# A retention and channel-mix kernel on one core: its steps in a new order, the last columns halved, the first load in one transfer, ten zero products for twelve

## The chip, the cores and the metric

One core of a Trainium2 chip runs the whole kernel in one launch. The metric is the device time of one execution in microseconds. TensorE is PE below, VectorE DVE, ScalarE ACT, GpSimd POOL and SyncE SP; a weight load that belongs to a product is PEld.

## The reference, cut to what matters

Retention over 4 batches, 8 heads, 768 tokens and 64 columns a head, in blocks of 64 tokens, then a channel mix over the 512 columns of all heads:

```python
for b in range(12):                                    # blocks of 64 tokens
    intra = (qb @ kb.T * Dmask) @ vb                   # Dmask[i, j] = lam**(i - j) for i >= j
    out[block b] = intra + (qb * lam_pow) @ kv_state
    kv_state = lam**64 * kv_state + (kb * rev_pow).T @ vb
x_prev = x shifted by one token
xk = mu_k * x + (1 - mu_k) * x_prev                    # 512 columns
xr = mu_r * x + (1 - mu_r) * x_prev
k = relu(xk @ w_k)                                     # 1024 columns
r = sigmoid(xr @ w_r)
result = r * ((k * k) @ w_v)                           # 512 columns
```

The three weights arrive in float64, all else in float32.

## The kernel before, in words

**Tiling.** Two blocks make a stage of 128 tokens, so there are six stages n = 0 to 5. Heads are taken in pairs hp = 0 to 3, and all four batches go together. Attention gives x with its columns on partitions, one tile [128 columns, 4 x 128 tokens] a head pair. Weights, x and the squares of k are split into two parts, a high and a low one, and each product of the channel mix runs three times (`product`, `PASSES`): high by high, high by low, low by high.

**Attention** of a stage and head pair (short products of 64 x 64, 16 of a kind): `scores` (tile sc), `decay` (times the table Dt, DVE), `decay_queries`, `decay_keys` (ACT, in place in tile in or kin), `sums` (tile u), `even_state` and `odd_state` (the running state), `values` (tile xp). Then `mix_prev` and `mix` make xk and xr, and `split_x` the two parts (xh, xl). A stay in attention below is a run of such short products in PE's list, between long runs of the others: from stage 1 on mostly the values of two head pairs and the scores and sums of two others.

**Channel mix** of a stage: 48 products for r (`r_part`, tile rp, 6 by 4 rows of the order) and the sigmoid `r_out`; 96 for k (`k_part`, tile kp, eight tiles of 128 columns) with `k_square` and `k_split` (tile k); 96 for v (`v_part`, tile vp), whose result DVE multiplies by r (tile rt) and ACT's queue stores (`v_cols`). In stage 0 k is made head pair by head pair (`k_product`), as x comes. The last block of all (stage 5, batch 3) is computed and stored in two pieces of its columns (lines 462 and 463).

**Weights** come as float64 through SP's queue (`stage_part`, tile raw) and are turned into the two float32 parts on the chip, during stage 0: `conv_top` (ACT, tile top), `conv_bits` (DVE), `conv_split` (ACT writes wk, wr or wv, DVE the low part).

**Start.** The inputs of stage 0 come in pieces of a tile of 2048 columns for each head pair (keys twice, queries, values), cut at the columns of `CUTS` (line 503), issued by SP in the steps L, N and M (`load_first`). Small constants (smalls, eye) come first; from them DVE, POOL, ACT and PE make the table Dt and the tile LP (`powers`, steps T0 and T2). PE begins with products of zeros that nobody reads (`keep_busy`, step Z). Line 173 runs a Sigmoid on one column, with nothing behind it that reads the result.

**Order.** The string `ORDER` (from line 505) is the whole program: each word is a step, a letter (the table `steps`, lines 483 to 490), a stage, a tile or a weight, and a head pair or a part. Each step issues its instructions on their engines, and every operation goes through `InOrder` (line 25), which keeps each engine, and each queue, in the order of the program. So the order of this string is the order of each engine's list, and all instructions carry line 33. Loads are issued by SP (steps L, N, M, S), stores by ACT.

Of the kernel before, what the change touches and what calls it, by code (L numbers as in the profile page):

```python
# [7 lines left out]
F32 = mybir.dt.float32  # L8
F32R = mybir.dt.float32r
I32 = mybir.dt.int32  # L10
U32 = mybir.dt.uint32
# [3 lines left out]
AF = mybir.ActivationFunctionType  # L15
# [6 lines left out]
NF = DFF // 128  # L22
# [14 lines left out]
def tile_retention_moe(  # L37
# [25 lines left out]
    tensor, vector, scalar, gpsimd, sync = (  # L63
        InOrder(tc, e) for e in (tc.nc.tensor, tc.nc.vector, tc.nc.scalar, tc.nc.gpsimd, tc.nc.sync))
# [37 lines left out]
    def load_first(hp, part):  # L102
        cuts = CUTS[hp]
        part = min(part, len(cuts) - 2)
        if hp not in first:
            t = big.tile([128, 2048], F32, tag=f"big{hp}", name="in")
            first[hp] = t
            views((0, hp), [None] + [t[:, c * 512:c * 512 + 512] for c in (0, 2, 1, 3)])
        sync.dma_start(first[hp][:, cuts[part]:cuts[part + 1]], qvk0[hp, :, cuts[part]:cuts[part + 1]])
# [33 lines left out]
    one = tiny.tile([128, 1], F32, name="one")  # L143
# [10 lines left out]
    gpsimd.tensor_tensor(pows[:, 3:6], lam1.broadcast_to([128, 3]), ecol, op=ALU.pow)  # L154
    gpsimd.tensor_tensor(PW, lrow, prow.broadcast_to([128, H]), op=ALU.pow)
    gpsimd.tensor_tensor(KD, lrow, erow.broadcast_to([128, H]), op=ALU.pow)

    last, now, then = lam1, impulse, steps8
    for i in range(3):
# [10 lines left out]
    vector.tensor_tensor(rows.rearrange("p (c a) -> p c a", a=8), now[:, 8:25].rearrange("p (c o) -> p c o", o=1).broadcast_to([128, 17, 8]),  # L170
                         lows.rearrange("p (o a) -> p o a", o=1).broadcast_to([128, 17, 8]), op=ALU.mult)
    vector.tensor_scalar(omu, mus, -1.0, 1.0, op0=ALU.mult, op1=ALU.add)
    scalar.activation(one, one, AF.Sigmoid)
    gpsimd.memset(lastw, 0.0)
    gpsimd.tensor_copy(lone[:, 512:640].rearrange("p (a x) -> p a x", a=2),
                       parity.rearrange("p (a o) -> p a o", o=1).broadcast_to([128, 2, 64]))
# [231 lines left out]
    def product(p, stationary, moving, first, last):  # L408
        for i, (s, m) in enumerate(PASSES):
            tensor.matmul(p, stationary[s], moving[m], start=first and i == 0, stop=last and i == len(PASSES) - 1)  # L410

    def w_of(kind, i, c, cols):
        return [W[f"{kind}{i}"][:, c, s, cols] for s in (1, 0)]
# [43 lines left out]
    def v_part(n, i):  # L457
        b, half = divmod(i, 2)
        last = (n, b) == (NT - 1, B - 1)


        fs, cols = (range(half * 4, half * 4 + 4), slice(0, 512)) if not last else (
            range(NF), slice(half * 384, 384 + half * 128))
        if half == 0 or last:
            vps[n, b] = ps_m.tile([128, 512], F32, tag="m", name="vp")
        p = vps[n, b]
        for f in fs:
            x = k2[f // 2][:, f % 2, :, b * 128:b * 128 + 128]
            product(p[:, cols], [x[:, 0], x[:, 1]], w_of("v", f // 2, f % 2, cols),
                    f == 0, f == NF - 1)  # L470
        if last:
            v_cols(n, b, cols)

    def v_cols(n, b, cols):
        o = rt[b][:, cols]
        vector.tensor_tensor(o, vps[n, b][:, cols], o, op=ALU.mult)
        scalar.dma_start(out[b, n * 128:n * 128 + 128, cols], o)

    def v_out(n, b):
# [7 lines left out]
        y=lambda n, hp: split_x(n, 0, hp), x=lambda n, hp: split_x(n, 1, hp),  # L487
        M=lambda n, hp: load_first(hp, 2), b=keep_raw, G=lambda f, hp: k_product(0, f, hp),
        R=lambda n, hp: r_part(n, hp, 0), Q=lambda n, hp: r_part(n, hp, 1), s=r_out, K=k_part, h=k_square, p=k_split, V=v_part, o=v_out,
        S=stage_part, c=conv_top, C=conv_bits, D=conv_split)  # L490
    for step in ORDER.split():
# [8 lines left out]

CUTS = ((0, 1024, 1536, 2048), (0, 1536, 2048), (0, 1536, 2048), (0, 1536, 2048))

ORDER = """
L00 N00 M00 Z12 M02 T0 A00 a00 k00 B00 L02 Sk5 k02 Sk4 A02 b00 e00 E00 T2 a02 B02 F00 ck5 f00 L01 ck4 A01 Ck4 L03 x00 y00 e02
b02 Ck5 a01 Sk6 U00 Dk4 A03 M03 E02 a03 Dk5 Sk7 B01 u00 ck6 k03 G00 G20 e01 b01 Sk2 f02 Sk3 f01 ck7 E01 Ck7 G30 Ck6 B03 y01 y02
U02 Dk6 ck2 G10 G01 F01 G21 e03 b03 M01 Sr0 Sr1 f03 G31 Sr2 G11 ck3 k01 Ck2 G02 G22 G32 Ck3 Dk7 y03 Dk2 U01 u01 x01 G12 N11 G13
G03 Dk3 U03 cr0 Cr0 G23 h00 K07 Sr3 h01 F02 cr1 G33 E03 F03 Cr1 p00 h02 Dr0 cr2 h07 cr3 Cr2 Dr2 N10 Sv0 K05 x03 Sv3 Dr1 Cr3 h03
K06 K04 h06 x02 Sv1 p01 Dr3 q11 cv0 Q00 cv3 Cv0 h05 Cv3 h04 Dv0 L11 u03 cv1 Q01 u02 L10 Q02 Cv1 Dv3 Q03 k11 q10 R00 R01 Sv2 R02  # L510
R03 A10 s02 A11 k10 U11 Dv1 cv2 Cv2 U10 s00 p02 Dv2 V04 L12 p03 V02 s03 u11 a10 u10 k12 V05 N12 s01 a11 V03 L13 B11 B10 E11 w10
w11 N13 k13 A12 A13 e10 N21 N20 o02 o01 U13 U12 L21 E10 q12 L20 F11 u12 a13 V06 u13 q13 a12 V07 w13 k20 o03 V00 e11 f10 F10 w12
B13 x10 B12 A20 f11 k21 E13 x11 U21 A21 y10 U20 y11 L23 e12 e13 f12 F13 L22 V01 f13 y12 N22 y13 K13 N23 u21 q20 K15 E12 o00 k23
x13 h13 F12 w21 u20 q21 h15 K11 a21 K12 K14 a20 K10 k22 h14 p12 B20 x12 w20 h12 e20 f20 B21 A22 U22 q22 e21 U23 L30 h11 E20 A23
h10 F20 E21 Q10 Q11 Q12 Q13 u22 q23 w22 s12 f21 K17 F21 a23 p10 h17 u23 K16 R10 L31 s13 a22 R11 w23 y20 R12 R13 h16 x21 s10 k30
k31 B23 B22 N30 N31 p11 q31 A30 U30 A31 U31 y21 e23 E23 s11 F23 p13 L32 u30 e22 u31 N33 V10 f22 k32 V11 V14 a30 V15 f23 V12 x20
o10 L33 y22 V13 q30 y23 o12 K22 a31 x23 K25 E22 o11 K23 w31 h22 F22 K24 w30 N32 k33 V16 h23 V17 B30 h24 B31 U32 A32 h25 A33 q32
o13 U33 K27 x22 e30 e31 K26 f30 p22 N41 L40 E30 F30 K21 L41 h27 u32 u33 E31 K20 w32 f31 F31 h26 Q20 p21 Q21 h21 h20 k41 k40 Q22
Q23 q33 R20 R21 p20 a32 s22 V22 N40 w33 R22 a33 R23 y30 A40 p23 U40 U41 A41 s21 B32 y31 s20 q41 B33 s23 e33 f33 V23 V26 V27 x30
L43 o21 e32 a40 f32 y33 N43 E32 x31 V20 q40 u40 o23 y32 E33 V21 o20 F32 F33 K35 L42 h35 k42 Q30 N42 w40 Q31 K31 a41 h31 x33 V24  # L520
K34 u41 V25 x32 h34 p32 Q32 o22 K37 K30 w41 Q33 h37 h30 k43 B41 p30 e41 E41 B40 s32 E40 A43 f41 s33 U43 F40 A42 U42 u43 L51 K36
a42 N50 e40 f40 K33 q42 h36 R30 a43 h33 K32 u42 R31 q43 L50 N51 F41 k50 R32 R33 k51 B43 h32 p33 y40 p31 y41 s31 B42 s30 x40 E43
U50 e43 F43 U51 e42 x43 f42 y42 A51 f43 u51 A50 V32 L52 V33 y43 V36 o31 K44 V34 x41 N52 E42 F42 V37 q50 x42 K40 a51 h44 h40 o33
V30 V35 K41 u50 N53 V31 K45 h41 q51 h45 a50 p42 L53 w42 K47 o30 K46 p40 h47 K42 h46 Q40 h42 k52 o32 w43 K43 p43 B51 k53 h43 B50
e50 E51 f50 e51 A53 U53 f51 U52 E50 A52 Q41 y51 u52 Q42 F50 Q43 F51 R40 q53 R41 s43 p41 s42 R42 a52 x50 R43 s40 q52 V42 y50 s41
u53 V43 B52 a53 B53 e52 x51 f52 V46 E52 o41 F52 V47 e53 E53 y52 f53 V40 V44 V41 o40 y53 o43 V45 F53 K52 h52 R50 o42 K51 h51 K50
K53 x53 x52 R51 h53 h50 p51 R52 K54 K55 R53 h55 s50 s51 p50 h54 Q50 K57 p52 Q51 h57 V54 Q52 K56 h56 Q53 V50 p53 s52 V52 V53 V51
V55 s53 o51 o50 o52 V56 V57
"""


# [58 lines left out]
```

## Time and profile before

| | before |
|---|---|
| time, median of 3 runs | 403.63 us (403.32 to 403.79) |
| profiled execution | 403.18 us, its span 401.4 us |
| busy share of the span | PE 98%, PEld 81%, DVE 61%, ACT 51%, POOL 7% |
| chain that ended last | PE 86%, ACT 8%, DMA 4%, issue 1% |
| loaded and stored | 35.74 MB read, 6.29 MB written |
| granted TensorE clock, mean | 1.000 |

The span runs from the first to the last instruction, so the execution's own time is 1.8 us longer. Times in the rows are microseconds from the start of the span. The chain follows the work that ended last back to the start, from each piece to what released it. "issue" is time in which an engine waited for nothing that the profile shows. "SPq" and "ACTq" are an engine's DMA queue, L33 is line 33. A group of rows gives, for instructions of one kind, output <- inputs, count, busy time and mean duration, and the idle time before them with what ended it.

### The profile page before, as it was taken

How to read it: one execution, taken by the hardware profiler on the slowest of the kernel's cores; microseconds unless marked ns; L12 is line 12 of the kernel's file. 1: busy time of each engine (PE TensorE's matmuls, PEld its weight loads, DVE VectorE, ACT ScalarE, POOL GpSimd, SP SyncE). 2: the span in 40 equal slices, each digit the busy share in tenths (PEclk: the TensorE clock that was granted, in tenths of full speed). 3: DMA queues.
4: the chain of work that ended last, by engine and by line, in shares of the span. 5: the costliest groups of instructions: out<-in, count | busy, mean ns of one | idle time of the engine just before them, and what ended most of it. 6: DMA issues, size and time to landing. Idle time of an engine off the chain costs nothing.

```text
span 401.4 us, 8419 instructions
## 1 busy us (share of the span) xinstructions
PE 392.3 (98%) x3534; PEld 323.7 (81%) x3534; DVE 244.7 (61%) x392; ACT 206.0 (51%) x372; POOL 28.8 (7%) x100
## 2 busy tenths in 40 slices
PE   7899999899999999999999999999999999999997
PEld 3677877788888788888888888888888888888886
DVE  5897699887895783359575448755366941434111
ACT  5899998665657731186342445941237540224200
POOL 5221000010010100010100000000000000000000
PEclk9999999999999999999999999999999999999999
DMA  7999256927070710160261008080000000200011
GB/s 263 418 371 301 124 212 181 284 77 198 2 206 9 208 55 28 40 198 0 73 165 54 2 28 209 4 235 1 26 28 28 2 26 2 79 0 2 0 52 54
DMA packets 13318, 42.58 MB, mean 106 GB/s; under 512 B 1888, under 2 KB 2272, under 8 KB 13280
## 3 DMA queue, kind: packets, MB, share of 16 engines
q1 hardware_dynamic: 9536, 35.68, 28.5%
q10 hardware_dynamic: 3744, 6.36, 4.3%
q8 instruction: 28, 0.46, 0.5%
q14 instruction: 10, 0.08, 0.1%
HBM read 35.74 MB, written 6.29 MB: 105 GB/s over the span
## 4 chain that ended last, share of the span: by engine, by line
PE 86%; ACT 8%; DMA 4%; issue 1%; SPq 0%; DVE 0%; POOL 0%; ACTq 0%; POOLq 0%
PE vp L33 33%; PE kp L33 27%; PE rp L33 15%; PE xp L33 5%; DMA in<-qvk 4%; PE sc L33 3%; PE u L33 2%; ACT kf L33 2%; ACT top L33 2%; ACT xh L33 1%; ACT wk L33 1%; ACT ts L33 1%; ACT wr L33 0%; ACT in L33 0%; SPq L33 0%
## 5 line engine op out<-in xcount | busy, mean ns | idle before, releaser
L33 PE MATMUL vp<-wv,k 128*128 128x512 f32 (+2 forms) x600 | 136.0, 384 | 1.1 <-issue 1.1
L33 PEld LDWEIGHTS vp<-wv,k 128*128 128x128 f32 x600 | 110.0, 188 | 23.1 <-issue 1.4
L33 PE MATMUL kp<-xh,wk 128*128 128x512 f32 x384 | 123.0, 391 | 0.0
L33 PEld LDWEIGHTS kp<-xh,wk 128*128 128x128 f32 x384 | 72.1, 188 | 15.4 <-issue 0.2
L33 PE MATMUL kp<-xl,wk 128*128 128x512 f32 x192 | 74.9, 390 | 0.1
L33 ACT ACTIVATE kf<-kp 128x512 f32<-128x512 f32 x48 | 28.1, 594 | 75.9 <-PE kp L33 70.0
L33 PE MATMUL rp<-wr,xh 128*128 128x512 f32 x192 | 59.7, 392 | 0.2 <-ACT kf L33 0.2
L33 DVE TENSOR_TENSOR kf<-kf 128x512 f32<-128x512 f32 x40 | 27.1, 690 | 53.0 <-ACT kf L33 52.7
L33 DVE TENSOR_TENSOR xl<-ts,xh 128x512 fp32r<-128x512 f32 x48 | 32.6, 688 | 24.7 <-ACT xh L33 24.3
L33 ACT CAST xh<-ts 128x512 fp32r<-128x512 f32 x48 | 29.0, 617 | 30.4 <-DVE rt L33 26.2
L33 ACT COPY qv<-st 64x256 f32<-64x256 f32 x80 | 32.4, 405 | 20.6 <-DVE st L33 17.8
L33 PEld LDWEIGHTS rp<-wr,xh 128*128 128x128 f32 x192 | 35.6, 188 | 8.5 <-ACT kf L33 1.2
L33 PEld LDWEIGHTS kp<-xl,wk 128*128 128x128 f32 x192 | 36.1, 188 | 7.9 <-DVE xl L33 0.6
L33 DVE TENSOR_TENSOR k<-kf,k 128x1024 fp32r<-128x1024 f32 x24 | 29.4, 1224 | 15.6 <-ACT k L33 15.5
L33 DVE TENSOR_TENSOR mv<-qv,LP 64x256 f32<-64x256 f32 x80 | 33.6, 420 | 7.5 <-PE xp L33 5.9
L33 PE MATMUL rp<-wr,xl 128*128 128x512 f32 x96 | 37.4, 389 | 0.0
L33 ACT ACTIVATE ts<-xp,omu 128x512 f32<-128x512 f32 x43 | 28.4, 686 | 15.8 <-PE xp L33 9.1
L33 DVE TENSOR_TENSOR mv<-sc,Dt 64x512 f32<-64x512 f32 (+1 forms) x48 | 32.5, 685 | 3.2 <-ACT raw L33 2.0
L33 DVE SCALAR_TENSOR_TENSOR ts<-xp,smalls,ts 128x512 f32<-128x512 f32 x40 | 29.3, 747 | 6.7 <-ACT ts L33 6.4
L33 DVE TENSOR_TENSOR rt<-vp,rt 128x512 f32<-128x512 f32 (+2 forms) x25 | 16.6, 666 | 25.7 <-PE vp L33 25.5
L33 ACT CAST k<-kf 128x1024 fp32r<-128x1024 f32 x24 | 25.1, 1047 | 8.8 <-DVE kf L33 3.9
L33 POOL COPY ts<-lastw 128x4 f32<-128x4 f32 x48 | 14.9, 314 | 119.0 <-DVE xl L33 119.0
(65 smaller groups left out, 285.2 us busy)
## 6 DMA issues: line engine op xcount, KB each, us to landing
qv<-qv SPq DMA_DIRECT2D x40, 256.0 KB, 7.1
kin<-kk SPq DMA_DIRECT2D x20, 512.0 KB, 5.4
out<-rt ACTq DMA_DIRECT2D x23, 256.0 KB, 2.0
raw<-w_v SPq DMA_DIRECT2D x4, 1023.8 KB, 8.0
in<-qvk SPq DMA_DIRECT2D x3, 768.0 KB, 9.4
raw<-w_k SPq DMA_DIRECT2D x2, 1023.8 KB, 13.9
raw<-w_k SPq DMA_DIRECT2D x4, 511.8 KB, 9.5
raw<-w_r SPq DMA_DIRECT2D x4, 511.8 KB, 13.3
```

The source lines that it names most:

```text
L33: return lambda *args, **kw: self.tc.keep_in_program_order(op(*args, **kw))
```

## The change

Four edits. The string `ORDER` is written anew: every step of the old program is there (but for N00 and M00, which loaded the rest of the first tile), in another order throughout. The last block is cut 256 + 256 in place of 384 + 128. The first head pair's tile comes in one transfer of 1 MB, not in three. The Sigmoid on one column stands at the start of ACT's list, and there are ten zero products in place of twelve.

```diff
     gpsimd.tensor_tensor(KD, lrow, erow.broadcast_to([128, H]), op=ALU.pow)
+    scalar.activation(one, one, AF.Sigmoid)
...
     vector.tensor_scalar(omu, mus, -1.0, 1.0, op0=ALU.mult, op1=ALU.add)
-    scalar.activation(one, one, AF.Sigmoid)
     gpsimd.memset(lastw, 0.0)
...
         fs, cols = (range(half * 4, half * 4 + 4), slice(0, 512)) if not last else (
-            range(NF), slice(half * 384, 384 + half * 128))
+            range(NF), slice(half * 256, half * 256 + 256))
...
-CUTS = ((0, 1024, 1536, 2048), (0, 1536, 2048), (0, 1536, 2048), (0, 1536, 2048))
+CUTS = ((0, 2048), (0, 1536, 2048), (0, 1536, 2048), (0, 1536, 2048))
...
-L00 N00 M00 Z12 M02 T0 A00 a00 k00 B00 L02 Sk5 k02 Sk4 A02 b00 e00 E00 T2 a02 B02 F00 ck5 f00 L01 ck4 A01 Ck4 L03 x00 y00 e02
...
+L00 Z10 M03 Sk4 k03 T0 L02 ck4 k00 A00 T2 L01 a00 Ck4 Dk4 B00 b00 A02 M02 E00 a02 e00 M01 k02 k01 f00 A01 a01 B02 y00 Sk5 L03
...
```

**SP's loads at the start.** smalls are the constants, in the tiles of stage 0 (512 columns are 256 KB), raw the float64 weights. Before:

```order
L33 DMA smalls<-small 128x60
L33 DMA in<-qvk 128x1024
L33 DMA in<-qvk 128x512 x3
L33 DMA in<-qvk 128x1536
L33 DMA raw<-w_k 128x2047 x2
L33 DMA in<-qvk 128x1536 x2
```

and now:

```order
L33 DMA smalls<-small 128x60
L33 DMA in<-qvk 128x2048
L33 DMA in<-qvk 128x512
L33 DMA raw<-w_k 128x2047
L33 DMA in<-qvk 128x1536 x2
L33 DMA in<-qvk 128x512 x2
```

The first head pair's tile is one transfer; behind it comes the last quarter of pair 3 (step M03), then a weight.

**ACT at the start.** Dt are the copies of the table, in<-in,PW the key decays of stage 0 (two instructions a head pair), raw<-xp the copy of the first values, top<-raw a weight's first conversion. Before:

```order
L33 ACT_TABLE_LOAD
L33 ACTIVATE smalls<-smalls,pows 128x2
L33 ACTIVATE smalls<-smalls,pows 128x4
L33 ACT_TABLE_LOAD
L33 ACTIVATE one<-one 128x1
L33 COPY Dt<-table 128x32x4
L33 COPY Dt<-table 128x96x4
L33 ACTIVATE in<-in,PW 128x4x64 x4
L33 COPY raw<-xp 128x512
L33 ACTIVATE ts<-raw,omu 128x4x128 x2
L33 COPY LP<-table 128x256
```

and now:

```order
L33 ACT_TABLE_LOAD
L33 ACTIVATE one<-one 128x1
L33 ACTIVATE smalls<-smalls,pows 128x2
L33 ACTIVATE smalls<-smalls,pows 128x4
L33 ACTIVATE in<-in,PW 128x4x64 x2
L33 COPY Dt<-table 128x32x4
L33 COPY Dt<-table 128x96x4
L33 CAST top<-raw 128x512
L33 ACTIVATE in<-in,PW 128x4x64 x2
L33 COPY LP<-table 128x256
L33 CAST wk_196<-raw 128x512
L33 COPY raw<-xp 128x512
```

There is one table load, the key decay of pair 3 (step k03) stands ahead of the table's copies, and conversions and another key decay stand ahead of the copy of the first values.

**PE at the second stay in attention** (stage 1, between V products of stage 0; xp, sc and u are values, scores and sums, each row 16 products). Before:

```order
L33 MATMUL vp<-wv_744,k_2_741 128x512 x6
L33 MATMUL vp<-wv_619,k_3_761 128x512 x6
L33 MATMUL xp<-mv,qv_437 64x64 x16
L33 MATMUL xp<-mv,qv_511 64x64 x16
L33 MATMUL sc<-qv_805,kin 64x64 x16
L33 MATMUL sc<-qv_865,kin 64x64 x16
L33 MATMUL u<-qv_865,kin 64x64 x16
L33 MATMUL u<-qv_805,kin 64x64 x16
L33 MATMUL vp<-wv_597,k_0_493 128x512 x6
```

and now:

```order
L33 MATMUL vp<-wv_751,k_2_746 128x512 x6
L33 MATMUL vp<-wv_628,k_3_755 128x512 x6
L33 MATMUL xp<-mv,qv_515 64x64 x16
L33 MATMUL xp<-mv,qv_623 64x64 x16
L33 MATMUL vp<-wv_610,k_0_492 128x512 x6
L33 MATMUL vp<-wv_644,k_1_586 128x512 x6
L33 MATMUL sc<-qv_836,kin 64x64 x16
L33 MATMUL u<-qv_758,kin 64x64 x16
L33 MATMUL u<-qv_836,kin 64x64 x16
L33 MATMUL sc<-qv_758,kin 64x64 x16
L33 MATMUL vp<-wv_610,k_0_492 128x512 x6
```

Twelve V products stand between the values and the scores, and sums and scores change places.

## Rows read from the trace of the kernel before

**Rows 1.** The page, part 1: busy time, share and instructions of each engine.

```profile
PE 392.3 (98%) x3534; PEld 323.7 (81%) x3534; DVE 244.7 (61%) x392; ACT 206.0 (51%) x372; POOL 28.8 (7%) x100
```

**Rows 2.** Busy time by stretch, 20 to 52 us, under its line of columns.

```profile
core 0: us, PE busy (x) PEld busy (x) DVE busy (x) ACT busy (x) POOL busy (x), PEclk, DMA share, GB/s
20.00:52.00 32.00, 31.78 (x187) 24.75 (x185) 25.87 (x37) 31.36 (x51) 4.55 (x8) 1.00 0.77 269
```

**Rows 3.** The chain in order of time, three stays: start us, us, what.

```profile
74.58 0.43 PE vp L33
75.01 1.06 issue
76.06 8.21 PE vp L33 x35
...
107.64 2.02 PE xp L33 x64
...
111.68 5.75 PE rp L33 x24
...
130.32 0.62 PE sc L33 x32
...
132.23 0.64 issue
...
133.22 16.56 PE vp L33 x72
...
196.89 1.78 PE xp L33 x55
198.66 0.38 issue
...
199.55 13.84 PE vp L33 x60
```

**Rows 4.** Busy time by stretch, columns as in rows 2, between those places.

```profile
76.00:132.86 56.86, 56.17 (x759) 47.20 (x759) 45.64 (x79) 35.94 (x72) 5.73 (x21) 1.00 0.40 116
132.86:199.04 66.18, 65.79 (x635) 54.93 (x635) 40.24 (x67) 28.73 (x55) 3.80 (x14) 1.00 0.28 84
```

**Rows 5.** The page, part 3: queue, kind, packets, MB, share of the DMA engines.

```profile
q8 instruction: 28, 0.46, 0.5%
```

**Rows 6.** Groups by line and form: count, busy us, mean ns, idle before.

```profile
L33 PE MATMUL vp<-wv,k 128*128 128x384 f32 x24 | 4.3, 335 | 0.0
...
L33 PE MATMUL vp<-wv,k 128*128 128x128 f32 x24 | 2.8, 273 | 0.0
...
L33 ACT ACT_TABLE_LOAD x2 | 2.6, 1283 | 2.8 <-DMA smalls<-small 2.8
...
L33 DVE TENSOR_TENSOR rt<-vp,rt 128x384 f32<-128x384 f32 x1 | 0.6, 558 | 3.5 <-PE vp L33 3.5
...
L33 DVE TENSOR_TENSOR rt<-vp,rt 128x128 f32<-128x128 f32 x1 | 0.3, 292 | 2.0 <-PE vp L33 2.0
```

**Rows 7.** DMA issues: queue, operation, count, KB each, median us to landing.

```profile
in<-qvk SPq DMA_DIRECT2D x1, 512.0 KB, 4.9
out<-rt ACTq DMA_DIRECT2D x1, 192.0 KB, 1.9
out<-rt ACTq DMA_DIRECT2D x1, 64.0 KB, 1.6
```

**Rows 8.** Waits of ACT from 6 to 20 us: total, times, longest.

```profile
ACT raw L33 <- PE xp L33: 1.4, 1, 1.4
ACT Dt L33 <- PE table L33: 1.3, 1, 1.3
```

**Rows 9.** The timeline's start: start us, us, instruction, count, [wait and what ended it].

```profile
1.45 5.15 PE L33 MATMUL idle<-zeros 128*128 128x512 bf16 x12 [1.45 <-DVE zeros L33]
...
7.51 0.65 ACT L33 COPY Dt<-table 128x128 f32<-128x128 f32 x2 [1.32 <-PE table L33]
```

**Rows 10.** The chain of the first 30 us, columns as in rows 3.

```profile
2.11 5.28 DMA in<-qvk
...
7.41 12.13 DMA in<-qvk
```

More of the change, by code (lines that the diff above doesn't have):

```diff
@@ L498, in tile_retention_moe @@
             steps[step[0]](i if i in "rkv" else int(i), j)
-CUTS = ((0, 1024, 1536, 2048), (0, 1536, 2048), (0, 1536, 2048), (0, 1536, 2048))
+CUTS = ((0, 2048), (0, 1536, 2048), (0, 1536, 2048), (0, 1536, 2048))
 ORDER = """
-L00 N00 M00 Z12 M02 T0 A00 a00 k00 B00 L02 Sk5 k02 Sk4 A02 b00 e00 E00 T2 a02 B02 F00 ck5 f00 L01 ck4 A01 Ck4 L03 x00 y00 e02
-b02 Ck5 a01 Sk6 U00 Dk4 A03 M03 E02 a03 Dk5 Sk7 B01 u00 ck6 k03 G00 G20 e01 b01 Sk2 f02 Sk3 f01 ck7 E01 Ck7 G30 Ck6 B03 y01 y02
-U02 Dk6 ck2 G10 G01 F01 G21 e03 b03 M01 Sr0 Sr1 f03 G31 Sr2 G11 ck3 k01 Ck2 G02 G22 G32 Ck3 Dk7 y03 Dk2 U01 u01 x01 G12 N11 G13
@@ L509 @@
[L509 to L528, printed above, removed]
+L00 Z10 M03 Sk4 k03 T0 L02 ck4 k00 A00 T2 L01 a00 Ck4 Dk4 B00 b00 A02 M02 E00 a02 e00 M01 k02 k01 f00 A01 a01 B02 y00 Sk5 L03
@@ new lines @@
+ck5 F00 B01 e02 b02 Ck5 G30 A03 Sk6 f02 b01 G00 e01 G20 f01 a03 Dk5 ck6 Sk7 y01 Ck6 E01 Sk2 ck7 U00 u00 B03 G10 y02 Ck7 G01 G31
+x00 F01 e03 G21 Dk6 G11 b03 f03 G32 ck2 Dk7 Sk3 x01 Sr0 U01 Sr1 y03 Ck2 G12 E02 ck3 Ck3 u01 G02 G22 Sr2 G23 G13 E03 U03 F02 Dk2
+cr0 U02 Dk3 G33 G03 Sv3 h01 K05 cr1 h00 Cr0 Cr1 Sr3 cr2 F03 Dr0 p00 K06 Sv1 h03 cr3 Cr2 N10 Cr3 h02 q10 Dr2 K04 K07 x02 Dr3 h04
+Dr1 h05 x03 Q00 Q01 Sv0 L11 p01 cv0 Cv0 Q02 Q03 cv3 Cv3 h06 s02 Dv0 R00 cv1 Cv1 N11 u02 L10 Dv3 k10 Sv2 R01 k11 u03 Dv1 R02 R03
@@ new lines @@
+A10 s01 A11 a10 U11 U10 cv2 V04 Cv2 L12 p02 h07 Dv2 L13 p03 N13 u10 q11 V02 V05 u11 V03 s00 B10 k13 a11 N12 o01 B11 E11 w11 e10
+o02 e11 w10 V06 A12 E10 U13 q13 k12 q12 f11 F10 N20 U12 s03 A13 u12 a12 f10 u13 a13 x10 N21 w12 F11 L20 V00 k20 y10 L21 V07 w13
+B12 y11 N22 B13 A20 k21 A21 e12 U21 f12 y12 U20 e13 f13 L22 o03 x11 N23 y13 E12 F12 u20 V01 k22 o00 a20 K12 E13 F13 q21 K13 K15
+K14 h13 u21 q20 w20 B20 L23 a21 k23 w21 x12 h14 h15 h12 B21 U23 e21 q23 A23 E20 f21 F20 A22 U22 p12 e20 x13 K10 L30 h10 a23 K11
@@ new lines @@
+K17 f20 E21 L31 N31 p11 F21 K16 h11 q22 Q10 Q11 k30 Q12 y21 u22 a22 h17 h16 u23 R10 Q13 w22 k31 R11 s13 w23 p13 y20 x21 N30 A30
+U30 p10 A31 s12 U31 B23 L32 B22 E23 e23 f23 R12 R13 s11 F23 u31 k32 e22 V14 f22 y23 y22 V15 V12 s10 L33 K23 N33 a31 x23 E22 F22
+u30 q31 V16 x22 h23 a30 o12 V13 V10 o11 V11 K24 K22 q30 V17 o10 h22 k33 N32 h24 B31 E31 w31 w30 e31 B30 U33 N40 o13 U32 p21 A32
+F31 A33 K27 u32 K26 f31 a32 q32 u33 h27 h26 x20 N41 K25 p23 h25 E30 K20 Q20 e30 h20 F30 Q21 L41 K21 k41 L40 f30 Q22 a33 h21 Q23
@@ new lines @@
+y31 q33 y30 s23 R20 p22 x30 w33 R21 w32 B32 s22 k40 B33 e32 A41 U40 f32 U41 E32 N43 A40 e33 F32 f33 R22 y33 x31 R23 y32 K31 s20
+K30 s21 E33 p20 q40 V26 L42 u41 h30 u40 V27 x32 F33 o23 V24 q41 V25 Q30 h31 a41 V22 L43 Q31 k42 a40 w40 k43 x33 Q32 w41 Q33 o22
+V23 N42 V20 o21 A43 A42 U42 U43 s33 B41 p30 s32 E41 B40 N51 e40 f40 E40 F40 F41 V21 e41 a42 o20 K32 q42 K33 h33 u42 h32 K34 K37
+N50 L50 p31 L51 f41 h34 h37 K36 k51 K35 R30 u43 h36 q43 R31 R32 h35 a43 R33 p33 s30 B42 p32 x40 k50 B43 y40 q50 U51 A51 U50 s31
@@ new lines @@
+E43 A50 N53 V34 x41 e42 N52 E42 V30 u50 L52 V35 y41 e43 f42 L53 f43 F42 y42 V31 y43 V36 V37 a51 F43 q51 K41 o33 h41 K44 h44 V32
+u51 K42 w42 V33 a50 o30 K40 o31 x42 K45 k53 o32 k52 h40 p40 h45 x43 K46 B51 p42 B50 U52 h42 E50 w43 A53 e50 U53 h46 q52 f50 A52
+K43 K47 e51 q53 F50 h43 Q40 E51 F51 f51 p41 Q41 Q42 h47 u53 R40 R41 a53 y50 u52 R42 x50 R43 s41 Q43 s40 a52 p43 s42 V46 B53 B52
+y51 V47 s43 V42 e53 E53 e52 f52 f53 y53 F53 x51 E52 F52 V44 V45 V40 o43 V43 y52 K57 o42 K50 h57 o41 V41 x52 o40 K51 K56 h51 Q50
@@ L529 @@
+h50 K53 Q51 Q52 p50 h56 K54 x53 h53 p53 K52 h54 h52 Q53 K55 p51 s53 s52 V52 R50 R51 R52 h55 R53 s50 p52 s51 V54 V57 V53 V50 o51
+V51 V55 o50 o52 V56
 """
```

## The prediction

> **What bounds the kernel now.** I read the page's shares first, then the windows of the start, then the chain of waits from front to back, then the loads. PE is busy for 392.3 of 401.4 us with 3534 products and 3534 weight loads [rows 1], so the end is set by what PE is given and by where it stands still. Between 20 and 52 us PE is busy 31.78 and ScalarE 31.36 of 32 us [rows 2]: there both are full, and the little that PE waits for comes from ScalarE's conversions. From 52 us on the chain is PE alone, and the reader should look in it for the word "issue" [rows 3]: PE stands still though no engine, transfer or buffer holds it up.
>
> There are three such places, each in or just behind attention. **A:** 36 V products take from 74.58 to 84.27, 9.69 us; 60 of them elsewhere take 13.84, or 0.231 each, so 36 should take 8.3: 1.4 us lost. **B:** scores and sums of a stay take from 130.32 to 133.22, 2.90 us; in an undisturbed stay they follow the values that end at 107.64 + 2.02 = 109.66 and last until 111.68, 2.02: 0.9 lost. **C:** the values take from 196.89 to 199.55, 2.66, and in the stay at 107.64 only 2.02: 0.6 lost. Together 2.9 us [rows 3].
>
> What they have in common is their distance. From A's end to B's end PE gets 759 products and 759 loads, 1518 instructions, from B's end to C's 1270 [rows 4]. With the 18 and 10 waits that stand in PE's list in between these are 1536 and 1280, that is 6 and 5 times 256. The queue named "instruction" moved 28 packets, 0.46 MB [rows 5]; 28 times 256 is 7168, and PE's list has some 7140 instructions. So each packet is the next 256 instructions of PE, and A, B and C stand exactly at such seams, before instruction 1473, 3009 and 4289. An attention product is short: 256 instructions of scores and sums pass in 2.02 us, 256 of V products, at 0.231 for a product with its load, in 30 us. From the first instruction of a block until the next block is there it takes, by A (2.0 + 1.4), B (2.1 + 0.9) and C (2.7 + 0.6), 3.0 to 3.4 us. A block that is used up faster than that makes PE stand still; any other seam is free.
>
> The Trainium skill, "Runtime: NRT & Kernel Launch", section Instruction fetch mechanics, also has blocks of 256 instructions, but says that the cost of crossing one is "mostly hidden". By that rule the new order would gain nothing at the seams. Rows 3 disagree at three seams of 27, and the measurement decides.
>
> **The change, part by part.** *Seams in attention.* I counted the new list as I counted the old one. In the second stay 12 V products now stand between values and scores, other stays begin with scores, others put sums first; each stay still has the same instructions. The seam before 1473 now falls in scores that have 6 V products (1.4 us) and 240 short instructions (1.9) in their block: 3.2 us, against 3.0 to 3.4 needed, so 0 to 0.2 lost. The seam before 3009 has 4.7 us, that before 4289 5.6. One block lies badly, from 4545 to 4801: it is one stay's scores and sums, 2.0 us, right behind V products. If its successor were asked for only at its first instruction, 1.0 to 1.4 would be lost; but V products ahead of it are slow, and if the successor is asked for only five of them (1.2 us) earlier, nothing is lost; no row here shows how early that is. I take 0.2 there and 0.1 at 1473. So this part gives -2.9 + 0.3 = **-2.6 us**, bounds -2.9 and -1.3.
>
> *Last columns.* The last block's 48 products were 24 of 384 columns, 4.3 us, and 24 of 128, 2.8 us [rows 6]; now all 48 have 256. No row has that width. From both sides: 0.179 (384 columns) and 0.117 (128) each, so 5.6 to 8.6 us instead of 7.1. From 512 columns (0.231, above) to 384 the price falls by 0.052; on that line 256 columns cost 0.127, and 128 would cost 0.075, where the row has 0.117: so the line bends below 256, and I take 0.127, nearest to the row of 128. 48 x 0.127 = 6.1, so -1.0. Behind the last product VectorE now has 256 columns, between 0.29 and 0.56 us [rows 6], 0.13 more than before; the store has 128 KB between 64 KB (1.6) and 192 KB (1.9) [rows 7], 0.1 more. Together **-0.8**, bounds -1.3 and +1.7; the first half's VectorE work and store hide under the second half's products.
>
> *Start.* Up to the first r product both lists give PE the same 96 k products and the same attention of the first 128 tokens, and ScalarE the same conversions; only their order differs. As ScalarE is full from 20 us on [rows 2], and waits before that (6 to 20 us) only twice for over 1 us [rows 8], the start ends later or earlier by what it idles there. Removed: one of two table loads, 1.28 us [rows 6], and two zero products, 0.86 of 5.15 [rows 9]. ScalarE waits 1.3 us for the table products behind the one [rows 8], PE for the first load behind the other, so both count nothing; without that cover they would bring what they take. Moved: ScalarE's first real work was the decay table's copies at 7.51 [rows 9]; now the key decay of head pair 3 stands before them and waits for the second transfer. Today the first 512 KB, issued at 1.2, has landed at 6.1 (4.9 us [rows 7]), and the first 1 MB by 2.11 + 5.28 = 7.39 [rows 10]: 0.65 us for 256 KB, so the next 256 KB would be there at 8.0. So ScalarE begins 0.5 later. On the other side it waits 1.4 us for the first values today [rows 8], and in the new list a conversion and a key decay stand where that wait is. The first pair in one transfer lands between 6.1 and 7.4, and today the table products keep PE until 7.4 anyway, so nothing is lost by waiting for all of it. The later loads move the same bytes. I take **0**, bounds -1.4 (that wait gone) and +1.4 (0.5 later and a wait as long elsewhere).
>
> *Elsewhere* the order of all steps is new, but PE's products are the same, ScalarE and VectorE are busy 51% and 61% of the span [rows 1], and I find no place where a product's input is made less than a stay ahead. PE gets to everything sooner by what is saved; the loads are issued when PE frees a buffer, so they move with it.
>
> **Sum:** -2.6 - 0.8 + 0 = -3.4. The profiled execution took 403.18 us, so it would take 399.8; the median of the three runs shown is 0.45 above it, which makes **400.2 us**.
>
> **Rivals.** *1. The seams are not cured* (chance 0.10): a load in flight delays a packet, and blocks that last 3 to 5 us stop PE as A to C do now. For it: A, where loads were in flight, lost most. Against it: B and C had none to speak of. Only the tail is gained, and 0.2 at the seams: 402.6. This is also what the rule of the skill quoted above would give.
> *2. The start gains as well* (0.12): ScalarE's 1.4 us wait goes and the first load lands early: 400.2 - 1.4 = 398.8.
> *3. PE's clock rises late* (0.04). The twelve zero products take 0.43 us for 512 columns [rows 9], the 1.2 GHz level; V products at 0.231 are the 2.4 GHz level. Now the zeros end 0.86 us sooner and PE then waits for the load. If the level stayed low until 25 us, some 18 products would cost 0.2 more each, +3.6: 403.8, no change. Against it: table products follow the zeros at once. The Trainium skill ("TensorE: Matmul & The Clock Gate", What you observe) has it that activity lifts the clock, which makes this possible and gives no price here.
> *4. Slower* (0.04): the second transfer does not land in order but shares the queue with what follows, as the one issued at 7.41 that landed 12.13 us later [rows 10]. ScalarE's list stands still at pair 3's key decay, and behind it wait the table's copies, VectorE's first decay and all values of block 0. From a landing at 11.4 us on, 3.4 late, the gain is gone, from 12.2 on it is slower; at 13.8 (8.0 + 5.8) it is 406.0. Against it: 512 KB at 6.1 and 1 MB at 7.4 (above) are transfers that landed one behind the other.
>
> **Numbers.** The forecast has 0.70. A measurement of this kernel can tell 0.2%, 0.8 us, from no change, so "faster" means below 402.8. Faster: the forecast, rival 2 and half of rival 1, 0.87. Within 0.2%: the rest of rival 1 and rival 3, 0.08. Slower: rival 4 and what I have not seen, 0.05. For the range the bounds of the three parts do not all fall together: from 398.5 (rival 2, a little early) to 402.5 (rival 1, or a start at its worst bound with one seam uncured).
>
> **What would show it.** Right: the chain from 52 us on has no "issue" of more than 0.2 us; every stay has 2.02 us for values and 2.02 for scores and sums; 48 products of 256 columns take about 6 us; the first r product comes within a us of today's; one table load. Wrong: "issue" rows at a seam (rival 1); k products of 0.43 us after 20 us (rival 3); ScalarE idle at the first key decay beyond 8.5 us (rival 4); 256-column products at 0.15 us or more.

## The result, and the profile after

The changed kernel takes **399.15 us** (median of 4 runs, 398.97 to 399.48), the kernel before beside it 403.68 (403.32 to 403.79): 4.5 us less, ratio 0.989 (95% interval 0.9873 to 0.9907). The profiled executions took 403.18 and 399.15 us, 4.0 apart, their spans 401.4 and 397.3, 4.1 apart. The experiments ran later, where single runs spread more (the kernel before: medians of 403.4 to 403.6, runs from 402.4 to 405.9), so there I read a median with its interval and, for the mechanism, the profile.

The page of the changed kernel, part 1, answers to [rows 1]:

```profile
PE 389.7 (98%) x3532; PEld 321.5 (81%) x3532; DVE 244.6 (62%) x392; ACT 204.2 (51%) x371; POOL 29.9 (8%) x100
```

The chain in order of time (start us, us, what), which answers to [rows 3]:

```profile
50.81 5.06 PE rp L33 x21
...
69.00 2.02 PE xp L33 x64
71.02 2.94 PE vp L33 x12
73.96 0.62 PE sc L33 x32
74.59 0.96 PE u L33 x58
75.61 0.34 PE sc L33 x22
75.95 0.20 issue
76.15 0.35 PE sc L33 x9
76.50 5.69 PE vp L33 x24
...
157.60 2.72 PE vp L33 x12
...
223.30 1.09 PE sc L33 x64
224.39 0.93 PE u L33 x64
225.32 2.02 PE xp L33 x64
...
374.58 19.38 PE vp L33 x108
393.99 0.42 DVE rt L33
```

One "issue" is left from 52 us on. The stay at 73.96 lasts until 76.50, 2.54 us where an undisturbed one takes 2.02: 0.5 lost, where A, B and C had lost 2.9. That is the seam before 1473. The stay at 223.30, whose scores and sums are the block from 4545 to 4801, takes 2.02: nothing lost.

ScalarE's waits from 6 to 20 us, which answer to [rows 8], and its busy time by stretch, from its first work on a tile to where the first r products wait for the last time, 50.81 in the changed kernel and 52.11 before (columns as in [rows 2]; the second fence is the kernel before, of which this stretch was not shown):

```profile
ACT in L33 <- DMA in<-qvk: 4.1, 1, 4.1
ACT top L33 <- DMA raw<-w_k: 0.5, 1, 0.5
...
7.60:20.00 12.40, 10.18 (x107) 7.38 (x106) 9.81 (x16) 11.70 (x24) 3.09 (x10) 1.00 1.03 416
20.00:50.81 30.81, 30.45 (x195) 23.97 (x194) 27.07 (x37) 30.59 (x50) 4.57 (x8) 1.00 0.83 300
```

```profile
7.51:20.00 12.49, 10.12 (x132) 8.02 (x133) 9.65 (x17) 10.81 (x23) 2.15 (x9) 1.00 1.02 414
20.00:52.11 32.11, 31.79 (x188) 24.75 (x186) 25.98 (x37) 31.44 (x52) 4.55 (x8) 1.00 0.77 270
```

ScalarE does the same work in both, 11.70 + 30.59 = 42.29 us and 10.81 + 31.44 = 42.25, but in 43.21 and in 44.60 us. So it idles 0.9 us instead of 2.35, and PE runs on alone from 50.81 rather than 52.11. The first scores of stage 1, which stand behind the first 24 r products, show the same step in the timeline (start us, us, instruction; first the kernel before, then the changed one):

```profile
57.09 1.16 PE L33 MATMUL sc<-qv,kin 64*64 64x64 f32 x64
55.80 1.16 PE L33 MATMUL sc<-qv,kin 64*64 64x64 f32 x64
```

These starts vary: in the profiles of the experiments they are 57.3 and 57.7 for two more kernels with the old start, and 55.7 to 56.4 for six more with the new one (four in which loads or conversions at the start are altered are not counted; they come below).

The last columns and stores, by line and form and among the DMA issues, answer to [rows 6] and [rows 7]:

```profile
L33 PE MATMUL vp<-wv,k 128*128 128x256 f32 x48 | 6.1, 283 | 0.0
...
L33 DVE TENSOR_TENSOR rt<-vp,rt 128x256 f32<-128x256 f32 x2 | 0.8, 425 | 5.7 <-PE vp L33 5.7
...
out<-rt ACTq DMA_DIRECT2D x2, 128.0 KB, 1.7
```

**Where the 4.1 us of span went.** The start gives 52.11 - 50.81 = 1.3. From there to the last 108 V products it is 325.98 us before (52.11 to 378.09) and 323.77 now, 2.2 less: 2.4 from the stalls, 0.2 given back, because the 12 V products set between values and scores take 2.94 us where 12 in a longer run take 2.72. (Two pieces of 0.2 us more cancel: the scores at 72.33 in the kernel before, and the r products at 304.13 in the changed one.) The last 108 V products take 19.38 where they took 20.43, 1.05 less. From there to the end of the span it is 3.3 us where it was 2.9, 0.45 more. 1.3 + 2.2 + 1.05 - 0.45 = 4.1.

### The profile page after: what moved, and what is told of

Its sections match the earlier page's. It is cut to its first block, busy times and chain, and to the rows that moved or that the text cites. A ratio compares the mean times of both kernels' runs of the same rounds, so it can differ in the third digit from the quotient of the medians.

```text
span 397.3 us, 8399 instructions
## 1 busy us (share of the span) xinstructions
PE 389.7 (98%) x3532; PEld 321.5 (81%) x3532; DVE 244.6 (62%) x392; ACT 204.2 (51%) x371; POOL 29.9 (8%) x100
## 4 chain that ended last, share of the span: by engine, by line
PE 86%; ACT 7%; DMA 4%; DVE 1%; issue 0%; SPq 0%
PE vp L33 33%; PE kp L33 28%; PE rp L33 15%; PE xp L33 5%; DMA raw<-w_k 3%; PE sc L33 3%; PE u L33 2%; ACT top L33 2%; ACT kf L33 2%; DMA in<-qvk 1%; ACT xh L33 1%; ACT wk L33 1%; ACT wr L33 1%; ACT k L33 0%; ACT ts L33 0%
## 5 line engine op out<-in xcount | busy, mean ns | idle before, releaser
L33 PE MATMUL vp<-wv,k 128*128 128x512 f32 (+1 forms) x600 | 135.0, 382 | 0.0
L33 DVE TENSOR_TENSOR rt<-vp,rt 128x512 f32<-128x512 f32 (+1 forms) x25 | 16.7, 667 | 37.8 <-PE vp L33 37.7
L33 ACT ACTIVATE ts<-xp,omu 128x512 f32<-128x512 f32 x42 | 27.5, 686 | 21.3 <-PE xp L33 9.9
L33 ACT ACTIVATE rt<-rp 128x512 f32<-128x512 f32 x24 | 14.1, 597 | 28.9 <-PE rp L33 15.4
```

The lines of the kernel that those rows point to most:

```text
L33: return lambda *args, **kw: self.tc.keep_in_program_order(op(*args, **kw))
```

## The experiments

Three questions: are the stalls a matter of where the seams fall, or of the stays; what in the start gives 1.3 us; and does anything do better.

**Every seam 64 instructions earlier in the new order.** `keep_short` is new, with a step z:

```diff
+    def keep_short(count):
+        for _ in range(count):
+            tensor.matmul(idle[0:32, 0:32], zeros[:, 0:32], zeros[:, 512:544], start=True, stop=True)
...
-L00 Z10 M03
+L00 Z6 z36 M03
```

> The new order as it is, but at PE's start 6 long zero products and 36 short ones (32 columns, read by nobody) in place of 10 long ones: 64 instructions more, so every seam of 256 instructions falls 64 earlier in the work, and nothing else changes. Theory (seams of instruction packets): the seams before 1921, 2433, 2945 and 4225, counted in the new kernel's list as it was, now fall in stays, each in a block that is used up in 2.7 to 3 us where about 3.8 are needed; PE stands still about 1.0, 1.2, 0.9 and 0.9 us there with 'issue' in the chain, and the 0.4 us of the changed kernel goes: 399.15 + 3.6 = 402.7 us (402.0 to 404.0). Rival (the gain comes from the order of the stays, or from what DVE and ScalarE do behind it, not from where the seams fall): the same time as the changed kernel, 399.2 us within 0.5, and no issue longer than 0.4 us.

Measured: 404.25 us (ratio to the kernel before 1.0025, 1.0005 to 1.0046), all of the gain and more gone, and 0.25 us above the range expected. Its chain:

```profile
85.15 0.92 PE u L33 x61
86.07 1.99 issue
88.06 0.33 PE u L33 x3
...
105.83 0.46 PE u L33 x30
106.29 0.78 issue
107.06 0.33 PE u L33 x2
...
128.70 1.31 PE xp L33 x38
130.01 0.46 issue
130.47 0.97 PE xp L33 x25
...
193.93 0.27 PE sc L33 x17
194.20 0.60 issue
194.80 0.46 PE sc L33 x15
```

Four stalls at the four seams named. By the whole chain these runs of short products last 4.33 (from 84.06), 3.12 (104.27), 2.74 (128.70) and 2.89 us (192.37) instead of 2.02, so 2.3 + 1.1 + 0.7 + 0.9 = 5.0 us are lost; the first is far more than the 1.0 expected of it. Part 3 of its profile, for 85.5 to 86.0 us alone (queue, packets, MB, share), has the packet; from 80 to 85.5 it has none, and from 84.0 to 85.5 it has the second line, loads that fill the DMA engines:

```profile
q8 instruction: 1, 0.02, 14.6%
q1 hardware_dynamic: 119, 0.43, 101.7%
```

So the packet starts when scores and sums are three quarters through, and PE goes on, at 88.06, some 2.5 us later. That second interval hardly varies: in the three stalls of the kernel before, the four here and the one of the changed kernel, PE goes on 2.3 to 2.9 us after its packet starts. What varies is when the packet starts. Ahead of this one and of A's, at 73.3, loads were moving; ahead of B's, C's and the other three here, none, and those stalls cost less. No run tests the loads alone. No step of the work moved; the rival falls.

**Every seam 188 earlier in the old order.**

```diff
-L00 N00 M00 Z12 M02
+L00 N00 M00 Z5 z101 M02
```

> The kernel before, its order untouched, but at PE's start 5 long zero products and 101 short ones (32 columns; 31 ns each in the run with 36 of them) in place of 12 long ones: 188 instructions more in about the same time, so every seam falls 188 earlier in the work. Counted on the old trace, no seam then lies in a stay. Theory (seams): none of the three stalls is left, no issue above 0.2 us in the chain from 52 us on, 2.3 to 2.8 us less than the kernel before on the same chip: about 401.1 us. Rival (the stalls belong to the old order's stays, through what DVE, ScalarE or the transfers do there): stalls of 1.3, 0.8 and 0.5 us stay where they are in the work, the time of the kernel before within 0.5 us.

Measured: 401.91 us, ratio 0.9955 (0.9943 to 0.9968), 1.7 less. Its chain at the places of A and C, and in the stay behind A's:

```profile
67.04 7.07 DMA qv<-qv
...
75.77 8.39 PE vp L33 x36
...
87.28 0.13 issue
...
196.24 2.02 PE xp L33 x64
198.25 13.85 PE vp L33 x60
```

A, B and C are gone, with no order changed (B's scores and sums, from 130.53 to 132.56, take 2.03 us). The gain is a third smaller than expected, and the profile has two reasons. A load issued at 67.04 lands at 74.11 and PE's scores wait for it, as the list of waits has it (in us, times, longest):

```profile
PE sc L33 <- DMA qv<-qv: 0.7, 1, 0.7
```

And one seam does lie in a stay, against the count: the scores and sums from 86.18 to 88.68 take 2.50 us, 0.5 lost around the "issue" at 87.28, and PE goes on 2.6 us after a packet's start. In the next experiment, which has the old order and the old seams, the same load costs 0.6 us and A then only 0.6: the two lie one behind the other, and a PE that stands still for the load may well give the packet time. Taking A away gains less where that load is late.

**The tail alone**, in the kernel before.

```diff
-            range(NF), slice(half * 384, 384 + half * 128))
+            range(NF), slice(half * 256, half * 256 + 256))
```

> The kernel before, with only the last block cut 256 + 256. From the two traces: the 48 products give 1.0 us, the work behind the last product costs 0.4 more: 403.7 - 0.5 = 403.2 us, with the three stalls of before unchanged. The prediction's sum would give -0.8: 402.9. Rival (the end is set by the store alone): 403.7 or more.

Measured: 402.87 us, ratio 0.9975 (0.9961 to 0.9990), 0.7 less. The interval holds both sums. The chain of its end, against 20.43 us before:

```profile
378.57 19.36 PE vp L33 x108
```

1.07 us less for the products, and from the last product to the end of the span (401.1) 3.2 us, 0.3 more. In this profile seams 1473, 2497, 3009 and 4289 all stopped PE, for 0.6, 0.4, 0.6 and 0.4 us: 2497 had stopped it for next to nothing in the kernel before. With margins near zero the same seam stops PE in one execution and not in the next.

**The new start before the old rest.** Prefix up to R00 in the new order with Z12, then all other steps in the old order:

```diff
-CUTS = ((0, 1024, 1536, 2048), (0, 1536, 2048),
+CUTS = ((0, 2048), (0, 1536, 2048),
...
-L00 N00 M00 Z12 M02 T0 A00 a00 k00 B00 L02 Sk5 k02
+L00 Z12 M03 Sk4 k03 T0 L02 ck4 k00 A00 T2 L01 a00
```

> All steps up to the first r product in the new order (with the first load in one transfer, but 12 zero products and the Sigmoid at its old place), all steps behind it in the old order, the old last block; PE's list has the same number of instructions up to the first r product, so the seams fall where they fell before. Theory (ScalarE's idle time of 1.4 us in the old start is what the new start gains): first r product about 1.3 us earlier, at 50.8, the three stalls of 1.3, 0.8 and 0.5 us unchanged: 402.4 us. Rival (the start gains by the zero products or the table load that went): 403.7 us. If the three stalls went with the new start: 399.7.

Measured: 402.78 us, by the medians 0.8 less, but the ratio is 0.999 (0.997 to 1.001), an interval that takes in no change. The profile is plainer. The first scores of stage 1 were at 57.09 in the kernel before, at 55.80 in the changed one, and here:

```profile
55.69 1.16 PE L33 MATMUL sc<-qv,kin 64*64 64x64 f32 x64
```

1.4 earlier, with twelve zeros and two table loads, and no wait for values. The stalls stay, though not the same three (1473, 2497 and 4289, with the starts of neighbouring products 1.16, 0.59 and 0.60 us apart; 3009 costs 0.3), and 0.6 us goes to the late load again.

**ScalarE's gap opened again in the new start.**

```diff
-L02 ck4 k00 A00 T2 L01 a00 Ck4 Dk4 B00 b00 A02 M02 E00 a02 e00 M01
+L02 k00 A00 T2 L01 a00 B00 b00 A02 M02 E00 a02 e00 ck4 Ck4 Dk4 M01
```

> The changed kernel with one thing of its start taken back: the first weight conversion (ScalarE 0.77 us, then its two parts) no longer stands ahead of the copy of the first values but behind that block's two mixes; loads and PE's list are untouched. Theory (the new start gains because ScalarE has work where it waited 1.4 us for the first values): ScalarE idles 0.8 to 1.4 us ahead of that copy again, first r product at 51.6 to 52.2 in the chain in place of 50.8, 399.2 + 1.0 = 400.2 us. Rival (the gain is the earlier load or the shorter zeros): 399.2 us, no new wait.

Measured: 401.77 us (400.26 to 403.33 in 12 runs), ratio 0.9957 (0.9938 to 0.9976); the profiled execution took 400.51. Its timeline:

```profile
11.24 0.58 ACT L33 COPY raw<-xp 128x512 f32<-128x512 f32 x1 [1.05 <-PE xp L33]
```

```profile
57.22 1.16 PE L33 MATMUL sc<-qv,kin 64*64 64x64 f32 x64
```

The wait is back, 1.05 us, and the first scores start 1.4 later than in the changed kernel. One weight's conversion in the right place is worth the whole gain of the start; why the median lies 1.3 us above the profiled execution, and 1.6 above what was expected, is open.

**The gap filled in the old start.**

```diff
-L00 N00 M00 Z12 M02 T0 A00 a00 k00 B00 L02 Sk5 k02 Sk4 A02 b00 e00 E00 T2 a02 B02 F00 ck5 f00
+L00 N00 M00 Z12 M02 Sk5 T0 A00 a00 k00 B00 L02 k02 Sk4 A02 ck5 b00 e00 E00 T2 a02 B02 F00 f00
```

> The kernel before with two steps moved: the first half weight is asked for one transfer earlier and its conversion on ScalarE (0.77 us) stands ahead of the copy of the first values, where ScalarE waits 1.4 us. Theory (what the start gains is ScalarE's idle time filled): the wait shrinks to about 0.6 us, first r product 0.5 to 0.8 us earlier than the kernel before, 403.6 - 0.7 = 402.9 us. Rival (the end of the start is set by the weights' arrival): no change, 403.6.

Measured: 405.4 us, ratio 1.0049 (1.0032 to 1.0066): 1.8 more in place of 0.7 less, a miss. PE's longest wait in the start:

```profile
PE sc L33 <- DMA in<-qvk: 2.3, 1, 2.3
```

The copy waits no more, but the weight now passes before pair 2's tile, whose scores stand in PE's list ahead of the first sums; PE waits 2.3 us and the first scores of stage 1 start at 59.41. I had counted ScalarE's list and left out the queue that the load was moved past.

**The three small edits of the start.** All three undone together:

```diff
-L00 Z10 M03
+L00 N00 M00 Z12 M03
...
-    scalar.activation(one, one, AF.Sigmoid)
...
+    scalar.activation(one, one, AF.Sigmoid)
```

(with the old CUTS, and the Sigmoid back at line 173.)

> The changed kernel with its three small edits at the start undone: first head pair in three transfers, twelve zero products, Sigmoid at its old place (second table load). Seams move by 4 or 5 instructions. Theory (all three hidden: PE and ScalarE wait for the first load and for the key decay of pair 3 anyway): 399.2 us within 0.4, first r product within 0.3 us of 50.8. Rival (they bring what they take, 1.28 + 0.86 us, at least in part): 400.0 to 401.3 us.

Measured: 399.96 us (399.58 to 401.50), ratio 0.9913 (0.9887 to 0.9938). In the profiled execution, at 401.5, VectorE and then PE waited for a load of stage 1 that took 10.5 us to land, which is none of the edits' doing; so the edits once more, in two parts:

> The changed kernel with the first head pair's tile in three transfers again. Theory (hidden: the same bytes in the same order, and ScalarE waits for the second transfer behind them): 399.2 us within 0.4; the key decay of pair 3 starts within 0.3 us of 7.6. Rival (one transfer is what lets the rest land earlier): 400 us or more, key decay of pair 3 at 8.0 or later.

> The changed kernel with twelve zero products and the Sigmoid at its old place. Theory (both lie in ScalarE's wait of 4.1 us for the first load): 399.2 us within 0.4. Rival (they bring what they take): 400.0 to 401.3 us.

Measured: 399.60 (399.25 to 400.41) and 399.61 us (399.40 to 401.35), ratios 0.9904 and 0.9909. The changed kernel itself was run again as well, at another time than these:

> The changed kernel itself, beside the others on this chip: 399.2 us by its first measurement; 399.2 to 399.9 if this chip's loads are as uneven as in the last runs.

Measured: 399.25 us, ratio 0.989 (0.9876 to 0.9904). So by the medians each part is 0.35 us above the changed kernel and all three 0.7, and the intervals, which overlap, don't tell that from nothing. With the old cuts the key decay of pair 3 starts later, though:

```profile
8.06 0.91 ACT L33 ACTIVATE in<-in,PW 128x256 f32<-128x256 f32 x2 [4.61 <-DMA in<-qvk]
```

It starts at 7.60 in the changed kernel, 0.46 us sooner, as the rival there had it. But with all three edits undone it starts at 7.90, and in the other profiles with the single transfer at 7.56 to 7.79: one transfer instead of three brings the second tile 0.1 to 0.5 us sooner. The first scores of stage 1, 56.50 here, lie just behind the 55.7 to 56.4 of the single transfer. That profile had no stall at 1473, which gave 0.4 us back.

**No zeros at all.**

```diff
-L00 Z10 M03
+L00 M03
```

> The changed kernel without any zero product: every seam falls 20 instructions later, that before 1473 just behind its stay. Theory (seams, and a start set by ScalarE): the stall of 0.4 us shrinks or goes, PE's first products run at 1.2 GHz for longer but end before ScalarE wants them: 398.8 to 399.4 us. Rival (without zeros the granted level of 2.4 GHz comes late and PE, not ScalarE, sets the start): 16 attention products take over 1.3 us after 10 us, first r product later by 1 us or more, 400.5 us or more.

Measured: 399.49 us (399.13 to 399.83), ratio 0.9897. PE's timeline:

```profile
4.78 1.97 PE L33 MATMUL table<-eye,rows 128*128 128x128 f32 x8 [4.78 <-DVE rows L33]
6.68 1.77 PE L33 MATMUL sc<-in 64*128 64x128 f32 x16
...
11.20 1.16 PE L33 MATMUL sc<-in 64*128 64x128 f32 x16
```

Table products and first scores run slowly (1.77 us; the same scores take 1.16 later), but PE is back at its pace by 11.2 us, and the first scores of stage 1 come at 55.94, between the 55.80 and 56.05 of the changed kernel's two profiles. The zeros are worth nothing that these runs can show. The stall at the seam did not shrink: with the seam just behind its stay, scores and sums are its block, and 0.6 us were lost. I expected the opposite, and this is a miss.

**V products moved ahead of the stay.**

```diff
-w10 V06 A12 E10
+w10 V06 V00 A12 E10
...
-L20 V00 k20
+L20 k20
```

> The changed kernel with 12 V products moved from behind the stay at 74 us to ahead of it, so the seam before 1473 falls 24 instructions earlier in the stay, in a block with 12 more V products. Theory (a block that lasts longer than the packet needs costs nothing): the block lasts 5.5 us rather than 3.5, the stall of 0.4 us goes: 0.4 us less than the changed kernel on the same chip, 398.8 us. Rival (what stops PE there is the late packet after a load, however long the block): the stall stays, 399.2.

Measured: 403.82 us, ratio 1.000 (0.9981 to 1.0019). Its chain:

```profile
74.91 0.50 ACT rt L33
75.41 0.04 issue
75.45 3.06 PE vp L33 x12
...
86.68 1.15 PE xp L33 x32
```

The seam no longer stops PE, as the theory has it, but the time expected, 398.8, is missed by 5 us. The profile, of an execution of 402.81 us, shows 3 us of it: V00 needs a buffer that a sigmoid frees (ACT rt until 75.41), PE waits 0.9 us for it and, before 86.68, 2.1 us for a mix (tile ts) that has become late. What the seam gave was lost many times over. No kernel tried beats the changed one.

## Why the prediction was right, and where it was off

The time, 399.15, lies within the range, 1.05 under the forecast of 400.2. The parts measured add to -4.1, not -3.4, which is most of it. The other 0.4 is no part of the kernel: the forecast added 0.45 because the median before lay that far above the profiled execution, and in the changed kernel it does not. That the sum came nearer than its parts is luck: the start gained 1.3 more than forecast, and three misses of about 0.2 the other way took half of that back.

*Seams* (forecast -2.6): right in mechanism and nearly in size, -2.4. Moving the seams with no step moved takes the stalls away or brings them back, which shows that the seams cause them. Of the two doubtful seams 1473 cost 0.5 where I took 0.1; its block, counted at 3.2 us (the two parts counted there add to 3.3), would have needed some 3.7, over the 3.0 to 3.4 that A to C gave. 4545 to 4801 cost nothing where I took 0.2: the trace has that packet at 220.4 us, 2.9 ahead of the stay, while slow products ran. The Trainium skill's rule that crossing a block is "mostly hidden" ("Runtime: NRT & Kernel Launch", Instruction fetch mechanics) agrees with most seams here and not with those inside stays, which cost 5.0 us in the shifted kernel.

*Last columns* (-0.8): products -1.05, as summed; behind them +0.45 where I had 0.23, so -0.6. VectorE (0.42 against 0.29) and the store (1.7 against 1.6) came as forecast; the other 0.2 lies between the store's landing and the end of the span and is not explained.

*Start* (0): this step failed. Its rule held: ScalarE is full, and the start ends by what it idles. The lower bound, -1.4, came nearly true, at -1.3. The two items for which the prediction had rows, the wait of 1.4 us that goes and a start 0.5 us later, add to -0.9; I took 0, setting against them a wait as long elsewhere, for which I had no row. But in one transfer the first tile and the next quarter came by 7.6, so ScalarE started 0.1 later, and the new wait was 0.5. This is rival 2's mechanism (chance 0.12, 398.8 us); the opened gap shows that it is the conversion ahead of the copy that does it, and the old cuts that the single transfer, which I had at nothing, may help by up to half a us on ScalarE.

*Elsewhere* (0): +0.2 for V products set into a stay. I did not price the change between long and short products.

*Rivals.* 1 (seams not cured) falls with the chain; but what it rests on, that loads in flight delay a packet, fits the traces, as the 2.3 us stall of the shifted kernel shows. 3 (the clock): PE without any zeros loses nothing that shows, so the 0.86 us of zeros could not matter. 4 (pair 3 late): the second transfer was there at 7.6. (In the chances, the rest of rival 1 and rival 3 add to 0.09, not 0.08.)

## What to carry to other kernels

Where the chain says "issue" on a busy engine and no wait explains it, count that engine's instructions between two such places: if they come out as multiples of one number, short instructions are outrunning their fetch, and a few harmless instructions ahead of them move the seams and show it. A run of short instructions is safe when it holds no seam, or when slow ones keep the engine busy until some 3 us after the packet for its next block has started; where loads are moving, that packet can be late, so leave more. And where an engine is full, sum its idle time in the old order and in the new: that, not the edits one by one, is what a new start is worth; count the load queue along with it.

## What was not expected of the hardware

A seam's cost is not fixed. The same seam before 1473 in the old order cost 1.4, 1.1, 0.9 and 0.6 us in four profiles, and one stay lost 2.3 us to a single seam where 1.0 was expected (the shifted kernel, 86 us). Most margins counted here were good to about half a us, that one was off by 1.3.
